# Reordering the first output stage, the first gate products and GpSimd's memsets in a windowed-attention and gated feed-forward kernel

## Chip, core and metric

The kernel runs on one core of a Trainium2 chip. Its time is the device time of one execution in microseconds (us); lower is better. TensorE (PE) does matrix products, VectorE (DVE) and ScalarE (ACT) work on their results in PSUM, GpSimd (POOL) casts, copies and clears in SBUF and issues some loads, SyncE (SP) issues the other loads, the stores and the transposing transfers.

## What is computed

```
scores = q k^T / 8                       # 8 batches x 8 heads, 576 tokens, head size 64
heads 0-3: keep 0 <= i-j < 32
heads 4-7: keep 0 <= i-j < 128 and (i-j) % 4 == 0
x = softmax(scores) v                    # to 4608 tokens x 512
out = (gelu(x w_gate) * (x w_val)) w_out # 512 -> 1536 -> 512
```

Inputs and output are float32; the products run on float16.

## The kernel before

**Units.** Two heads of one batch are one attention unit; unit n belongs to batch n // 4, and units of a batch are plain (heads 0-3) or dilated (heads 4-7). Unit n's steps have letters: S scores (TensorE), P exponential (ScalarE), M mask multiply (VectorE), D denominators and N numerators (TensorE), A or T and B the reciprocal of the denominators (A: two ScalarE passes, `lg` and `rb`; T, B: VectorE), X the multiply that writes x transposed into `xT[pair(n)]` (VectorE, L627). Unit 7 is the last unit of batch 1 and writes `xT[3]`.

**Chunks.** The feed-forward part goes over nine chunks of 512 tokens. A chunk has a gate stage and an output stage. The gate stage has 12 column blocks of 128; each takes four products of 128x512 for the gate and four for the value (`ffn1_part`, L636, one for each `xT`), then `g` (ScalarE, GELU, L801) and `u` (VectorE, L806). Blocks use two pairs of PSUM banks in turn, 0, 1 and 2, 3. The output stage has four blocks of 128 tokens with 12 products each (`ffn2`, L643) and a store (`e`: ScalarE copies, SyncE sends). The 12 products of a block use `wo` in three pieces, four products each.

**Order.** The order on all engines is written out by hand. `gates[c]` and `outs[c]` are strings of words: a number issues so many feed-forward products, and a word such as `S6@2+S7@6` issues steps of units with the PSUM place that they use (for D and N, 0 is banks 4 and 5, 1 is banks 6 and 7 in chunk 0's output stage). Attention of the next batch is thus laid between the output stage's products. `firsts[c]` gives the order of the first 16 gate-stage products, each as block, gate (0) or value (1), and which `xT`. `out_list` gives the order of output products and `out_banks` their banks.

**Loads.** `load_w` and `load_wo` issue the weights from GpSimd's queue. `load_first` (word F) loads q and k of a batch to `stage` from SyncE's queue and casts them on GpSimd (L221 plain heads, L233 dilated heads); `load_rest` (word H) transposes them by transfer (L273), loads v, copies k into block form on GpSimd (L289, L281, L327) and casts v (L262). [...] In chunk 0's output stage the word `V1` calls `second_v`: clear two tiles of batch 2, set `ones_two`, cast batch 1's v, and clear v tiles of batches 2 and 3 (`zero`, L206). A gate on the v loads of batch 1 lets them start once the second piece of `wo` has landed.

Of the kernel before, what the change touches and what calls it, by code (L numbers as in the profile page):

```python
# [21 lines left out]
def kernel(  # L22
# [22 lines left out]
    NNB = DFF // P  # L45
# [102 lines left out]
    def load_w(*parts):  # L148

        for i in parts:  # L150
            for t, w in ((wg_t, moe_w_gate), (wv_t, moe_w_val)):
                src = w[:, WC[i][0] : WC[i][1]].rearrange("(kc p) n -> p kc n", p=P)
                nc.gpsimd.dma_start(out=t[i], in_=src)  # L153

    def load_wo(i):
        return nc.gpsimd.dma_start(  # L156
            out=wo_t[i], in_=moe_w_out[i * CH : (i + 1) * CH, :].rearrange("(fc p) m -> p fc m", p=P)
        )
# [9 lines left out]
    def sixes(src, b):  # L168

        return src[b, 0:HK, :, :].rearrange("h (p r) d -> p h (r d)", r=6)  # L170

    def load_eights(b, pairs=((0, HK),)):
        for h0, h1 in pairs:
            for t, src in zip(eight(b), (q, k)):
                rows_ = src[b, HK + h0 : HK + h1, :, :].rearrange("h (p r) d -> p h (r d)", r=8)
                nc.gpsimd.dma_start(out=t[:, h0:h1].rearrange("p h r d -> p h (r d)"), in_=rows_)  # L176

    def blocks(t, plain):

        return t[:, (1 - plain) * 2 * NB2 * P : (2 - plain) * 2 * NB2 * P].rearrange("p (e c) -> p e c", c=P)  # L180

    def views(b):

        raw = qraw[b % 2]
        kt = raw[:, 1280 + 8 * NCL :]
        return (
            raw[:, 0:1280].rearrange("p (g c) -> p g c", g=2),
            raw[:, 1280 : 1280 + 8 * NCL].rearrange("p (g r i) -> p g r i", g=2, r=4),
            blocks(kt, 1),
            blocks(kt, 0),  # L190
            blocks(vraw[b % 3], 1),
            blocks(vraw[b % 3], 0),
        )
# [5 lines left out]
    def zero(t, eng=nc.gpsimd, gs=(0, 1), swap=1):  # L199

        for x in range(2):
            g = gs[0]
            part = t[64 * x : 64 * x + 64].bitcast(F32)
            first = 32 - 32 * (x ^ (g * swap))
            step = NB2 * 64 + swap * (32 if x else -32) * (1 - 2 * g)
            eng.memset(at2(part[:, NB2 * g], first, [[step, len(gs)], [64, NB2], [1, 32]]), 0.0)  # L206

    def st_of(i):
        return stage[:, 1280 * i : 1280 * i + 1280]
# [46 lines left out]
    def cast_v(dst, i, gs=(0, 1), swap=1):  # L256

        st = st_of(i)[:, 0:1152].rearrange("p (e d) -> p e d", d=D)
        for g in gs:
            for x in range(2):  # L260
                at = slice(NB2 * g, NB2 * g + NB2)
                nc.gpsimd.tensor_copy(dst[half_of(x), at, half_of(x, g * swap)], st[half_of(x), at])  # L262

    def half_of(x, swap=0):
        y = x ^ (1 if swap else 0)
        return slice(64 * y, 64 * y + 64)

    def odd(n):

        return n % 2 if n >= NHP else 0  # L270
# [370 lines left out]
    def ffn2(c, tb, bank, fcs):  # L641
        for fc in fcs:
            nc.tensor.matmul(  # L643
                ps[:, bank, :],
                u_all[:, fc, tb * P : (tb + 1) * P],
                wo_t[fc // 4][:, fc % 4, :],
                start=(fc == 0),
                stop=(fc == NNB - 1),
            )
# [75 lines left out]
    def second():  # L725

        load_w(4)
        for t in views(1)[2:]:
            zero(t)
        for t, src in ((0, q), (1, k)):  # L730
            nc.gpsimd.dma_start(out=six[:, t].rearrange("p h r d -> p h (r d)"), in_=sixes(src, 1))  # L731
        load_w(5)
        load_eights(1)
        wo1 = [load_wo(i) for i in range(3)][1]
        two_masks()
        tiles["two", 1] = views(1)
        gate["dma"] = wo1
        load_v(1, 1, True)
        load_v(1, 2, False)

    def second_v():
        for t in views(2)[2:4]:
            zero(t)
        nc.gpsimd.memset(ones_two, 0.0)
        for x in range(2):
            nc.gpsimd.memset(ones_two[half_of(x), half_of(x, 1)], 1.0)
        cast_v(views(1)[4], 1)
        cast_v(views(1)[5], 2)
        for t in views(2)[4:] + views(3)[5:]:
            zero(t)  # L750
        zero(views(3)[4], gs=(1,))

    def gate_banks(c, nb):

        if c == 0 and nb < 2:
            return ((4, 5), (6, 7))[nb]
        low = ((0, 1), (2, 3))
        return low[(nb + c) % 2]
# [14 lines left out]
    def out_list(c, banks):  # L773
        order = [(tb, fc) for tb in range(4) for fc in range(NNB)]
        if c == 0:
            order[: 2 * NNB] = [(tb, 4 * i + fc) for i in range(3) for tb in range(2) for fc in range(4)]
        return [lambda tb=tb, fc=fc: ffn2(c, tb, banks[tb], fcs=(fc,)) for tb, fc in order]

    def out_banks(c):
        return gate_banks(c, 2) * 2 if c < 7 else (4, 5, 6, 7)  # L780

    def run_program(c, words, mms, banks):

        units = {"S": two_s, "M": two_m, "D": two_den, "N": two_num, "T": two_t, "B": two_b, "X": two_x, "A": two_a, "P": two_p_of, "t": turn_first, "c": cast_six, "W": idle, "b": bias_first}
        joint = {"S": two_s_mms, "D": two_den_mms, "N": two_num_mms}
        for word in words.split():
            kind, args = word[0], [] if "+" in word else [int(x) for x in word[1:].split("@") if x]
            if "+" in word:
                lists = []
                for part in word.split("+"):  # L790
                    n, at = (int(x) for x in part[1:].split("@"))
                    lists.append((joint[part[0]](n, at), odd(n)))
                emit_tiles(*lists)
            elif kind.isdigit():
                for _ in range(int(word)):
                    mms.pop(0)()
            elif kind in units:
                units[kind](*args)
            elif kind == "g":
                g = ffn.tile([P, CH], F16, tag="g")  # L800
                nc.scalar.activation(g, ps[:, gate_banks(c, args[0])[0], :], AF.Gelu)  # L801
                tiles["g", args[0]] = g
            elif kind == "u":
                nb = args[0]
                val = ps[:, gate_banks(c, nb)[1], :]
                nc.vector.scalar_tensor_tensor(u_all[:, nb, :], tiles.pop(("g", nb)), USCALE, val, ALU.mult, ALU.mult)  # L806
            elif kind in "ew":
                at = args[1] if len(args) > 1 else c
                store(at, args[0], out_banks(at)[args[0]], "act" if kind == "e" else "dve")
            elif kind == "L":  # L810
                mms.clear()
                last_block(c, 3, banks[3])
            elif kind == "V":
                second_v() if args else second()
            elif kind == "F":
                load_first(args[0])
            elif kind == "H":
                load_rest(args[0])
            elif kind == "R":
                load_rest(3)  # L820
                load_first(4)
                load_rest(4)
            elif kind == "E":
                nc.scalar.preload_act_table_set("natural_log_exp_and_others")
            else:
                nc.scalar.preload_act_table_set("gelu_and_others")
        assert not mms
# [7 lines left out]
        ),  # L835
        1: (
            "5 N7@0 e3@0 F3 1 X7 1 G 7 g0 2 g1 1 u0 2 u1 2 g2 4 u2 4 g3 4 u3 4 g4 4 u4 4 g5 4 u5 4 g6 4 u6 4 g7 4 "
            "u7 4 g8 4 u8 4 g9 4 u9 4 g10 4 u10 4 g11 3"
        ),
        2: (  # L840
            "5 N11@1 e3@1 R 1 X11 G 7 g0 3 g1 u0 3 u1 2 g2 4 u2 4 g3 4 u3 4 g4 4 u4 4 g5 4 u5 4 g6 4 u6 4 g7 4 u7 "
# [23 lines left out]
    }  # L865
    outs = {
        0: (
            "V1 F2 S4@4+S5@6 1 E P4 10 P5 1 M4 S6@2+S7@6 M5 1 P6 3 D4@0 P7 M6 3 T4 2 e0@0 3 M7 1 e1@0 H2 2 B4 8 "
            "N4@1+D5@0 1 A5 X4 5 N5@0+D6@1 e2@0 1 A6 X5 5 N6@1+D7@0 1 A7 X6"
        ),  # L870
        1: (
            "1 u11 5 S8@0+S9@6 1 E P8 10 P9 M8 1 S10@0+S11@4 e0@1 M9 1 P10 4 P11 D8@1 M10 2 A8 1 M11 3 N8@0+D9@1 "
# [22 lines left out]
        ),  # L895
    }
    firsts = {
# [48 lines left out]
```

## Time and profile before

| | |
|---|---|
| median of 4 runs | 332.54 us (331.93 to 333.34) |
| profiled execution | 332.75 us, span 331.1 us |
| TensorE busy | 323.9 us of the span (98%) |
| VectorE, ScalarE, GpSimd busy | 150.9, 163.3, 149.5 us |
| 128x512 product, booked | 379 to 380 ns, 1284 of them |
| chunk 0: first gate product; first output product | 17.66 us; 42.73 us |
| chunk 1: first gate product; first output product | 56.63 us; 77.91 us |

Times in the profile are from the span's start. A row names the start, the busy time, the engine, the line, the operation with its operands and how many were merged; in brackets stands the idle time of the engine before it and what ended that idle time. The ends of matrix products are modelled. For transfers, SPq rows show the issue; the landing is reported apart, counted from the start of the issue.

### The profile page before, as it was taken

How to read it: one execution, taken by the hardware profiler on the slowest of the kernel's cores; microseconds unless marked ns; L12 is line 12 of the kernel's file. 1: busy time of each engine (PE TensorE's matmuls, PEld its weight loads, DVE VectorE, ACT ScalarE, POOL GpSimd, SP SyncE). 2: the span in 40 equal slices, each digit the busy share in tenths (PEclk: the TensorE clock that was granted, in tenths of full speed). 3: DMA queues.
4: the chain of work that ended last, by engine and by line, in shares of the span. 5: the costliest groups of instructions: out<-in, count | busy, mean ns of one | idle time of the engine just before them, and what ended most of it. 6: DMA issues, size and time to landing. Idle time of an engine off the chain costs nothing.

```text
span 331.1 us, 7540 instructions
## 1 busy us (share of the span) xinstructions
PE 323.9 (98%) x3040; PEld 158.4 (48%) x3040; DVE 150.9 (46%) x226; ACT 163.3 (49%) x246; POOL 149.5 (45%) x246
## 2 busy tenths in 40 slices
PE   7899999999999999999999999999999999999996
PEld 5654545444544454445544454444444444444443
DVE  6763654444443344344434459437743533303320
ACT  2663566535763577347733793356334543213322
POOL 8799877748445755736835941466000000000000
DMA  8999996797798999979789636965000110020002
GB/s 186 188 191 179 203 169 156 190 208 194 187 271 194 178 214 187 248 185 213 198 213 250 154 114 153 239 152 160 34 0 4 65 63 0 0 97 32 0 32 97
DMA packets 109027, 47.98 MB, mean 145 GB/s; under 512 B 83648, under 2 KB 104512, under 8 KB 108992
## 3 DMA queue, kind: packets, MB, share of 16 engines
q1 hardware_dynamic: 97216, 40.06, 51.4%
q0 software_dynamic: 11216, 6.79, 14.4%
q10 hardware_dynamic: 560, 0.66, 0.7%
q8 instruction: 24, 0.39, 0.5%
q14 instruction: 11, 0.09, 0.1%
HBM read 37.75 MB, written 9.44 MB: 143 GB/s over the span
## 4 chain that ended last, share of the span: by engine, by line
PE 85%; POOL 7%; DMA 7%; issue 0%; DVE 0%; POOLq 0%
PE ps L636 50%; PE ps L643 27%; PE ps L457 5%; DMA wo<-in_moe_w_out_dram 5%; DMA xT<-in_k_dram 2%; POOL wv L153 1%; PE ps L446 1%; POOL xT L176 1%; POOL wg L153 1%; POOL v L262 1%; PE ps L667 1%; POOL v L206 1%; POOL q L206 1%; POOL wo L156 0%; POOL s L731 0%
## 5 line engine op out<-in xcount | busy, mean ns | idle before, releaser
L806 DVE SCALAR_TENSOR_TENSOR u_all<-g,ps 128x512 f16<-128x512 f16 x108 | 73.6, 685 | 99.9 <-PE ps L636 92.9
L801 ACT ACTIVATE g<-ps 128x512 f16<-128x512 f32 x108 | 64.0, 598 | 109.2 <-PE ps L636 109.2
L636 PE MATMUL ps<-xT,wg 128*128 128x512 f16 x432 | 114.8, 379 | 0.2 <-DVE xT L627 0.2
L636 PE MATMUL ps<-xT,wv 128*128 128x512 f16 x432 | 113.3, 379 | 0.0
L643 PE MATMUL ps<-wo,u_all 128*128 128x512 f16 x420 | 98.8, 380 | 0.5 <-DMA wo<-in_moe_w_out_dram 0.5
L636 PEld LDWEIGHTS <-wv 128*128 128x128 f16 x432 | 42.1, 98 | 49.7
L636 PEld LDWEIGHTS <-wg 128*128 128x128 f16 x432 | 42.1, 98 | 49.7 <-issue 0.8
L643 PEld LDWEIGHTS <-u_all 128*128 128x128 f16 x420 | 38.3, 98 | 42.8 <-issue 0.8
L262 POOL CAST v<-stage 64x576 f16<-64x576 f32 x60 | 41.9, 698 | 8.5 <-DMA stage<-in_v_dram 5.6
L627 DVE TENSOR_TENSOR xT<-ps,rb 128x576 f16<-128x576 f32 x32 | 29.8, 940 | 23.3 <-PE ps L457 15.4
L221 POOL CAST s<-stage 128x640 f16<-128x640 f32 x24 | 16.9, 731 | 36.7 <-DMA stage<-in_q_dram 25.4
L508 ACT ACTIVATE P<-ps 128x832 f16<-128x832 f32 (+1 forms) x32 | 25.4, 836 | 15.1 <-PE ps L457 12.3
L654 ACT ACTIVATE osb<-ps 128x512 f32<-128x512 f32 x34 | 20.2, 595 | 20.4 <-PE ps L643 20.1
L289 POOL COPY q<-dense 64x1152 f16<-64x1152 f16 (+1 forms) x28 | 20.3, 726 | 15.3 <-DMA dense<-s 14.9
L281 POOL COPY q<-dense 64x512 f16<-64x512 f16 x28 | 17.1, 636 | 5.3 <-DMA dense<-s 3.7
L606 ACT ACTIVATE lg<-ps 128x576 f32<-128x576 f32 x23 | 15.0, 653 | 9.0 <-PE ps L457 8.6
L233 POOL CAST s<-stage 128x512 f16<-128x512 f32 x24 | 14.5, 631 | 9.7 <-DMA stage<-in_q_dram 6.1
L608 ACT ACTIVATE rb<-lg 128x576 f32<-128x576 f32 x23 | 15.8, 686 | 0.7
L513 DVE TENSOR_TENSOR P<-P,two_d 128x768 f16<-128x768 f16 x14 | 9.5, 682 | 13.8 <-ACT P L508 13.1
L513 DVE TENSOR_TENSOR P<-P,two_p 128x832 f16<-128x832 f16 x14 | 10.5, 760 | 11.2 <-ACT P L508 11.1
L457 PEld LDWEIGHTS <-v 64*64 64x64 f16 x460 | 9.2, 107 | 8.3 <-issue 7.0
L457 PE MATMUL ps<-P,v 64*64 64x96 f16 (+5 forms) x460 | 11.2, 199 | 0.0
(81 smaller groups left out, 181.4 us busy)
## 6 DMA issues: line engine op xcount, KB each, us to landing
out_dram<-osb SPq DMA_DIRECT2D x35, 256.0 KB, 2.8
stage<-in_v_dram SPq DMA_DIRECT2D x32, 144.0 KB, 3.6
stage<-in_v_dram SPq DMA_DIRECT2D x28, 128.0 KB, 3.1
stage<-in_q_dram SPq DMA_DIRECT2D x24, 128.0 KB, 3.9
stage<-in_k_dram SPq DMA_DIRECT2D x24, 128.0 KB, 2.9
stage<-in_q_dram SPq DMA_DIRECT2D x6, 512.0 KB, 4.5
stage<-in_k_dram SPq DMA_DIRECT2D x6, 512.0 KB, 5.3
wg<-in_moe_w_gate_dram POOLq DMA_DIRECT2D x6, 256.0 KB, 6.6
```

Source lines behind the costliest of these rows:

```text
L262: nc.gpsimd.tensor_copy(dst[half_of(x), at, half_of(x, g * swap)], st[half_of(x), at])
L281: eng.tensor_copy(dst[half, :, :, half_of(x, g)], src[half])
L289: nc.gpsimd.tensor_copy(out_, src[half].rearrange("p g (j c) -> p g j c", c=64))
L457: nc.tensor.matmul(o[cols], lhs[rows, cols], rhs[rows], start=st, stop=end, skip_group_check=True)
L508: nc.scalar.activation(pt[:, 0 : src.shape[1]], src, AF.Exp, bias=0.0, scale=scale)
L513: nc.vector.tensor_tensor(pt, pt, mask, ALU.mult)
L627: nc.vector.tensor_tensor(dst, num, rb, ALU.mult)
L636: nc.tensor.matmul(ps[:, bank, :], w[:, kc, ns], xT[kc][:, tok], start=first, stop=end)
L643: nc.tensor.matmul(ps[:, bank, :], u_all[:, fc, tb * P : (tb + 1) * P], wo_t[fc // 4][:, fc % 4, :], start=(fc == 0), stop=(fc == NNB - 1),)
L654: nc.scalar.activation(osb, ps[:, bank, :], AF.Copy, bias=0.0, scale=1.0 / USCALE)
L801: nc.scalar.activation(g, ps[:, gate_banks(c, args[0])[0], :], AF.Gelu)
L806: nc.vector.scalar_tensor_tensor(u_all[:, nb, :], tiles.pop(("g", nb)), USCALE, val, ALU.mult, ALU.mult)
```

## The change

It has five parts. In the gate stage of chunk 0, the value products of blocks 0 and 1 that need `xT[0]` and `xT[2]` go ahead of the products that need `xT[1]` and `xT[3]`. In the output stage of chunk 0, three token blocks instead of two go through the `wo` pieces together (36 products instead of 24), block 2 accumulates in bank 2 instead of bank 0, S6 is placed in banks 4 and 5 instead of 2 and 3, and the attention words and stores between the products move accordingly. In the gate stage of chunk 1, N7 is issued after 4 products instead of 5, and `xT[3]`'s first product becomes the twelfth instead of the thirteenth. The eight v memsets at the end of `second_v` become `blank_v`, which the new word `V2` calls after batch 2's `load_first` and ahead of its `load_rest`.

```diff
         cast_v(views(1)[4], 1)
         cast_v(views(1)[5], 2)
+
+    def blank_v():
         for t in views(2)[4:] + views(3)[5:]:
             zero(t)
         zero(views(3)[4], gs=(1,))
...
         if c == 0:
-            order[: 2 * NNB] = [(tb, 4 * i + fc) for i in range(3) for tb in range(2) for fc in range(4)]
+            order[: 3 * NNB] = [(tb, 4 * i + fc) for i in range(3) for tb in range(3) for fc in range(4)]
...
     def out_banks(c):
+        if c == 0:
+            return (0, 1, 2, 1)
         return gate_banks(c, 2) * 2 if c < 7 else (4, 5, 6, 7)
...
             elif kind == "V":
-                second_v() if args else second()
+                (second, second_v, blank_v)[args[0] if args else 0]()
...
     gates 1:
-            "5 N7@0 e3@0 F3 1 X7 1 G 7 g0 2 g1 1 u0 2 u1 2 g2 4 ...
+            "4 N7@0 1 e3@0 F3 1 X7 1 G 6 g0 3 g1 1 u0 2 u1 2 g2 4 ...
...
     outs 0:
-            "V1 F2 S4@4+S5@6 1 E P4 10 P5 1 M4 S6@2+S7@6 M5 1 P6 3 D4@0 P7 M6 3 T4 2 e0@0 3 M7 1 e1@0 H2 2 B4 8 "
-            "N4@1+D5@0 1 A5 X4 5 N5@0+D6@1 e2@0 1 A6 X5 5 N6@1+D7@0 1 A7 X6"
+            "V1 F2 S4@4+S5@6 1 E P4 10 P5 1 M4 S6@4+S7@6 M5 1 P6 5 D4@0 P7 M6 2 T4 5 M7 2 B4 1 e0@0 4 e1@0 V2 H2 "
+            "3 N4@1+D5@0 1 A5 X4 5 N5@0+D6@1 e2@0 1 A6 X5 5 N6@1+D7@0 1 A7 X6"
...
     firsts = {
-        0: "000 100 002 102 001 101 010 110 012 112 011 111 003 103 013 113",
-        1: "000 001 010 011 100 002 012 101 102 110 111 112 003 013 103 113",
+        0: "000 100 002 102 010 110 012 112 001 101 011 111 003 103 013 113",
+        1: "000 001 010 011 100 002 012 101 102 110 111 003 112 013 103 113",
```

More of the change, by code (lines that the diff above doesn't have):

```diff
@@ L836 @@
         1: (
-            "5 N7@0 e3@0 F3 1 X7 1 G 7 g0 2 g1 1 u0 2 u1 2 g2 4 u2 4 g3 4 u3 4 g4 4 u4 4 g5 4 u5 4 g6 4 u6 4 g7 4 "
-            "u7 4 g8 4 u8 4 g9 4 u9 4 g10 4 u10 4 g11 3"
+            "4 N7@0 1 e3@0 F3 1 X7 1 G 6 g0 3 g1 1 u0 2 u1 2 g2 4 u2 4 g3 4 u3 4 g4 4 u4 4 g5 4 u5 4 g6 4 u6 4 g7 "
+            "4 u7 4 g8 4 u8 4 g9 4 u9 4 g10 4 u10 4 g11 3"
         ),
```

## The prediction

> **What bounds the kernel now.** I read the page's totals first, then the waits of TensorE, then TensorE's own timeline around the three places that the diff touches, then the timelines of GpSimd and of SyncE's DMA queue from 50 to 80 us. The totals say that TensorE is the bound, and the granted clock is 1.00 in every stretch that I asked for:
>
> ```profile
> PE 323.9 (98%) x3040; PEld 158.4 (48%) x3040; DVE 150.9 (46%) x226; ACT 163.3 (49%) x246; POOL 149.5 (45%) x246
> ```
>
> So only a hole in TensorE's stream can be won, and a new hole costs in full. Between 15 and 80 us its waits are (us in total, times, longest):
>
> ```profile
> PE ps L643 <- DMA wo<-in_moe_w_out_dram: 0.5, 2, 0.2
> PE ps L446 <- ACT lg L606: 0.3, 1, 0.3
> PE ps L636 <- DVE xT L627: 0.2, 1, 0.2
> ```
>
> The timeline of TensorE shows these holes, and a fourth, before 60.65, that the list lacks; the ACT row beside it is its cause (start us, busy us, engine, line, operation, count, idle before):
>
> ```profile
> 18.81 0.81 PE L636 MATMUL ps<-xT,wg 128*128 128x512 f16 x3
> 19.77 0.59 PE L636 MATMUL ps<-xT,wg 128*128 128x512 f16 x2 [0.15 <-DVE xT L627]
> ...
> 42.73 1.90 PE L643 MATMUL ps<-wo,u_all 128*128 128x512 f16 x8
> 44.86 1.02 PE L643 MATMUL ps<-wo,u_all 128*128 128x512 f16 x4 [0.23 <-DMA wo<-in_moe_w_out_dram]
> 45.81 0.54 PE L457 MATMUL ps<-q 64*64 64x96 f16 x36
> 46.28 1.04 PE L643 MATMUL ps<-wo,u_all 128*128 128x512 f16 x4
> 47.16 0.52 PE L446 MATMUL ps<-P,two_ones 128*128 128x384 f16 x5
> 47.92 4.26 PE L643 MATMUL ps<-wo,u_all 128*128 128x512 f16 x19 [0.24 <-DMA wo<-in_moe_w_out_dram]
> ...
> 60.00 1.09 ACT L801 ACTIVATE g<-ps 128x512 f16<-128x512 f32 x2 [0.20 <-PE ps L636]
> ...
> 60.23 0.38 PE L636 MATMUL ps<-xT,wv 128*128 128x512 f16 x1
> 60.65 1.02 PE L636 MATMUL ps<-xT,wg 128*128 128x512 f16 x4
> ```
>
> **How large the holes are: a row against a rule.** The idle column gives 0.15 + 0.23 + 0.24 us, with some 0.04 before 60.65 that the chain shows as "issue": 0.66 us, 0.2% of the span. But one such product is booked at 379 ns, while 80 of them in the same gate stage start from 60.65 to 77.91: 0.2158 us each. The Trainium skill, "Perfetto Trace Analysis", section "Tensor Engine Instruction (MATMUL, LD_WEIGHTS)", says that a matmul's end in the profile is estimated from its size and not observed, so a difference of an end and a start is not the lost time. I count from start to start. Three products from 18.81 would let the next start at 19.46; it starts at 19.77: 0.31. Eight from 42.73 end at 44.46; next 44.86: 0.40. D4 with its change-over takes 0.37 (D8, a stage later: products due at 84.04 and 84.41), so after four products from 46.28 the next is due at 47.51; it starts at 47.92: 0.40. After 60.23 the next is due at 60.45; 60.65: 0.20. Sum 1.31 us. By the booked idle the change could win 0.66, by the starts 1.31; I take the starts.
>
> **The change, part by part.** No matmul, cast, memset or transfer is added or removed; all is order, but for two bank numbers and where eight memsets stand.
>
> Gate stage 0: four value and gate products of units 0 and 2 now stand before the first one of unit 1. Unit 1's X multiply starts at 18.96 and lasts 0.76, to 19.72. The product that waited for it is due at 19.46 + 4 x 0.2158 = 20.32: the 0.31 is gone. Unit 3's X ends at 20.74; its first product comes at 21.19. The values now start at 19.46 and need wv's first piece: issued 12.24, landed after 6.6, 18.84. Cover 0.6. Everything PE-paced after it is 0.31 earlier; the later weight pieces land earlier still, the nearest being k's eights (issued 30.11, 8.8 to landing: 38.9, needed from about 39.6).
>
> Output stage 0: before, 8 products use wo's first piece, then 8 and 8; now 12, 12, 12. The pieces are issued at 30.84, 31.62, 32.34 and land after 11.5, 13.2, 15.5: 42.3, 44.8, 47.9, and nothing in the change moves them. The first product is due at 42.42: on the edge, a wait of 0 to 0.1; I take 0. Twelve end at 45.01; S6 and S7 take 0.56 with their change-over (45.72 to 46.28 before). The second piece is needed at 45.5 (landed 44.8), six products go to 46.87, D4 to 47.24, six more to 48.5, and there the third piece is needed (47.9). Both 0.40 holes go. The first product of gate stage 1 moves from 56.63 to 56.63 - 0.31 - 0.80 = 55.52.
>
> New waits in this stretch. S6 moves from bank 2 to bank 4, so it waits for P4, and D4, which stands in bank 4 too, for P6; behind D4 in TensorE's queue stand 30 products. P4 and P5 end at 44.7 (45.0 less 0.31), S6 comes at 45.0, and S7 waited for P5 already. P6 began 0.66 after S6 in before and lasts 0.76: free 1.42 after S6; D4 comes 0.56 + 6 x 0.2158 = 1.85 after: cover 0.4. Block 2 in bank 2 meets only its own store, done before gate stage 1 wants the bank; block 3 in bank 1 starts 4 products and N4 after block 1's last product, 1.4 us, against a store of about 0.25 + 0.6. The thinnest cover is v: GpSimd's casts at 53.34 hang on SyncE's loads, which hang on wo's second piece and so do not move. The second of them ends at 54.72, and N6, before at 55.93, is now due at 54.82. The v casts of N4, N5 and N7 leave 0.8, 0.7 and 0.2. DVE hands X1 to TensorE in 0.05 (19.72 to 19.77), so the value is 0, the bounds 0 and 0.3.
>
> Gate stage 1: N7 and so X7 come one product earlier, product (0, gate, 3) is twelfth instead of thirteenth, and g0 is free to start 0.22 earlier against its stage. That product started at 59.59 and g0 at 60.00; now 58.27 and 58.68. The table load ended 0.21 before g0 in before, 58.67 now, so it just stops short of being the wait. g0 at 58.69 frees bank 2 at 59.34 (0.65 later, as before); the product that needs it is due at 59.34. The 0.20 is gone: 60.65 becomes 59.34. X7 ends 1.74 after N7's start, at 58.12, before 58.27.
>
> GpSimd's eight memsets, 4.36 us, go behind the q and k casts of batch 2. This wins nothing itself: it pays for what is late next. S8 needs the last copy of batch 2:
>
> ```profile
> 56.23 4.36 POOL L206 MEMSET v<- 64x576 f32 x8
> 60.65 2.81 POOL L221 CAST s<-stage 128x640 f16<-128x640 f32 x4
> ...
> 67.83 1.17 POOL L233 CAST s<-stage 128x512 f16<-128x512 f32 x2 [2.18 <-DMA stage<-in_k_dram]
> 71.64 2.34 POOL L289 COPY q<-dense 64x1152 f16<-64x1152 f16 x2 [2.63 <-DMA dense<-s]
> 75.73 1.16 POOL L281 COPY q<-dense 64x512 f16<-64x512 f16 x2 [1.75 <-DMA dense<-s]
> ...
> 78.64 0.29 POOL L327 COPY q<-q 128x128 f16<-128x128 f16 x1
> ...
> 60.25 0.55 SPq L228 DMA_DIRECT2D stage<-in_q_dram  x1
> 62.05 0.37 SPq L228 DMA_DIRECT2D stage<-in_k_dram  x1
> ```
>
> The copy ends at 78.93 and S8 starts at 79.30: cover 0.37. TensorE 1.31 earlier would find S8 0.9 short. Now walk the new order. q's plain pieces landed by 54.98 + 3.6 = 58.6, so their casts run 58.65 to 60.05. SyncE is ready for k's dilated load at 60.80; in before it stood there until the cast freed the stage at 62.03. It goes 1.2 us earlier, and in SyncE's queue the two stores and four transposes behind it go 1.2 earlier. Where q and k are issued 0.7 apart (89.9, 117.9, 145.2) they land 1.4 to 1.6 apart, here, 1.8 apart, 3.4. So k lands at 64.35 + 1.5 = 65.9, or, at its old 5.7, at 66.55. Casts to 67.1 (67.8); memsets, now in the idle time ahead of the copies, to 71.5 (72.2); plain copies to 73.9 (74.6); the last transpose, landed 75.7 before, 74.5 now; 3.2 more: last copy at 77.7 (77.8). S8 is due at 77.98. Wait 0, with bounds 0 and 1.1 (k landing at its old 67.75 puts the last copy at 79.0).
>
> Downstream nothing is near: batch 3's copies end at 108.4 for 114.1, and TensorE has no wait left after 60.65. VectorE and ScalarE are 46% and 49% busy. Sum: -0.31 - 0.40 - 0.40 - 0.20 = -1.31. The profiled execution took 332.75 (331.1 span and 1.65 around it), so 331.44; it stands 0.2 above the median of 332.54, so 331.2 against the median.
>
> **The rivals.** (a) Covers half fail: N6 waits for v, wo's first piece is late, the table load takes over as g0's wait, or S8 waits for its copy by up to 1.1. Total gain 0.2 to 0.9, 331.6 to 332.3. For it: four covers under 0.3 us in a row. Against: the moved chain is anchored to rows, and two routes to k's landing give the same end.
>
> (b) Slower: the memsets as GpSimd's new bound. They now stand between k's cast and S8's copies, so from k's landing L the last copy is at L + 0.05 + 1.2 + 4.4 + 2.4 + 3.2 = L + 11.25. From L = 66.7 S8 waits; at 68.0 the gain is used up; at 69.0 the kernel is 1.0 slower; at 69.7, 334.2. L = 69.0 is 8.1 us after issue. Against: the eight such loads I looked at landed 4.1 to 5.7 after issue.
>
> (c) The change doesn't do what it says in gate stage 0: another wait, such as the "ACT lg" one at 18.32 that the diff leaves alone, sets the time there, and the 0.31 stays. Then the gain is 1.0, 331.5. Against: X1 ends at 19.72 and the waiting product starts at 19.77, so the hole is X1's.
>
> **Numbers.** 1.31 whole or nearly: 0.66. Rival (a): 0.20. Rival (b): 0.10, nearly all of it past the point where it costs 1.0. Rival (c): 0.04, half to each side of the bound. A measurement of this kernel can tell about 0.3%, 1.0 us, from no change, so faster means below 331.54: 0.66 + 0.02 = 0.68; slower 0.09; same the rest, 0.23. The range: 330.7 (the sum and half a microsecond of the runs' own spread) to 332.4 (the upper end of (a)).
>
> **What would show it.** TensorE waits for wo and for xT gone; gate stage 1's first product at 55.5, the first product of gate block 2 at 59.3; the last GpSimd copy at 77.7 and S8 at 78.0; the tail 1.3 earlier. The forecast is wrong if N6 or S8 shows a GpSimd wait, or D4 an ACT one.

## The result and the profile after

The changed kernel takes 331.47 us (median of 42 runs, 330.88 to 333.05) against 332.62 us (64 runs). The ratio of the runs is 0.9974, with a 95% interval of 0.9967 to 0.9981: 0.86 us less, between 0.63 and 1.10. (The medians alone differ by 1.15.) Two more measurements beside the experiments gave 0.9975 both. The profiled execution took 331.48 us with a span of 329.8, which is 1.27 below the profiled execution of before (1.3 by the spans).

The page of the changed kernel, totals, and TensorE's waits between 15 and 80 us (us in total, times, longest). The L446 wait is in the prologue, at 15.6:

```profile
PE 322.9 (98%) x3040; PEld 158.1 (48%) x3040; DVE 152.0 (46%) x226; ACT 163.4 (50%) x246; POOL 150.2 (46%) x246
...
PE ps L643 <- DMA wo<-in_moe_w_out_dram: 0.3, 1, 0.3
PE ps L446 <- POOL v L262: 0.2, 1, 0.2
```

The timelines of TensorE and ScalarE at the same places as before; the PEld row is the weight load ahead of the product at 19.02:

```profile
18.29 0.81 PE L636 MATMUL ps<-xT,wg 128*128 128x512 f16 x3
19.02 1.04 PE L636 MATMUL ps<-xT,wv 128*128 128x512 f16 x4
19.01 0.55 PEld L636 LDWEIGHTS <-wv 128*128 128x128 f16 x4 [0.41 <-DMA wv<-in_moe_w_val_dram]
19.89 0.59 PE L636 MATMUL ps<-xT,wg 128*128 128x512 f16 x2
...
41.51 0.56 PE L457 MATMUL ps<-q 64*64 64x96 f16 x36
42.36 2.75 PE L643 MATMUL ps<-wo,u_all 128*128 128x512 f16 x12 [0.28 <-DMA wo<-in_moe_w_out_dram]
45.51 1.47 PE L643 MATMUL ps<-wo,u_all 128*128 128x512 f16 x6
46.81 0.52 PE L446 MATMUL ps<-P,two_ones 128*128 128x384 f16 x5
47.19 3.83 PE L643 MATMUL ps<-wo,u_all 128*128 128x512 f16 x17
...
58.70 1.22 ACT L805 ACTIVATE g<-ps 128x512 f16<-128x512 f32 x2
...
59.13 0.38 PE L636 MATMUL ps<-xT,wv 128*128 128x512 f16 x1
59.35 1.02 PE L636 MATMUL ps<-xT,wg 128*128 128x512 f16 x4
```

The four holes are gone: no product of the first gate stage waits for unit 1's X, the waits for the second and the third piece of `wo` do not occur, and gate block 2 starts at 59.35 with g0 at 58.70. Two waits are new. A small one: the first value product is due at 18.94 and starts at 19.02, because `wv`'s first piece, issued at 11.3, lands 7.7 later, at 19.0. A larger one: the first output product. S4 and S5 let the next product start at 42.00 (0.49 after their start, as in profiles without a wait), and `wo`'s first piece lands at 42.3 (issued 30.8, 11.5 to landing): 0.36 us of TensorE from start to start. The landings themselves did not move.

GpSimd, SyncE's queue and TensorE around S8:

```profile
58.91 1.38 POOL L221 CAST s<-stage 128x640 f16<-128x640 f32 x2 [2.69 <-DMA stage<-in_q_dram]
64.81 2.47 POOL L233 CAST s<-stage 128x512 f16<-128x512 f32 x4 [2.02 <-PE ps L636]
67.22 4.36 POOL L206 MEMSET v<- 64x576 f32 x8
71.62 2.32 POOL L289 COPY q<-dense 64x1152 f16<-64x1152 f16 x2
74.00 1.16 POOL L281 COPY q<-dense 64x512 f16<-64x512 f16 x2
76.92 0.29 POOL L327 COPY q<-q 128x128 f16<-128x128 f16 x1
...
60.31 0.37 SPq L228 DMA_DIRECT2D stage<-in_k_dram  x1
...
78.00 0.54 PE L457 MATMUL ps<-q 64*64 64x96 f16 x36
```

The memsets now fill the time in which GpSimd waited for the transposes. k's dilated load goes at 60.31 instead of 62.05, the last copy for S8 ends at 77.21 instead of 78.93, and S8 starts at 78.00 instead of 79.30.

### The profile page after: what moved, and what is told of

Read it like the earlier page. It is cut to its first block, busy times and chain, and to the rows that moved or that the text cites. A ratio compares the mean times of both kernels' runs of the same rounds, so it can differ in the third digit from the quotient of the medians.

```text
span 329.8 us, 7539 instructions
## 1 busy us (share of the span) xinstructions
PE 322.9 (98%) x3040; PEld 158.1 (48%) x3040; DVE 152.0 (46%) x226; ACT 163.4 (50%) x246; POOL 150.2 (46%) x246
## 4 chain that ended last, share of the span: by engine, by line
PE 86%; DMA 7%; POOL 4%; SPq 1%; issue 0%; DVE 0%; POOLq 0%
PE ps L636 50%; PE ps L643 29%; PE ps L457 5%; DMA wo<-in_moe_w_out_dram 3%; DMA stage<-in_v_dram 2%; DMA u_all<-in_q_dram 2%; PE ps L446 1%; POOL wv L153 1%; POOL wg L153 1%; PE ps L667 1%; POOL q L206 1%; POOL v L206 1%; SPq L245 1%; POOL xT L176 0%; POOL s L731 0%; POOL v L262 0%
## 5 line engine op out<-in xcount | busy, mean ns | idle before, releaser
L643 PEld LDWEIGHTS <-u_all 128*128 128x128 f16 x420 | 38.3, 98 | 42.3 <-issue 0.3
L262 POOL CAST v<-stage 64x576 f16<-64x576 f32 x60 | 41.7, 695 | 10.9 <-DMA stage<-in_v_dram 8.0
L221 POOL CAST s<-stage 128x640 f16<-128x640 f32 x24 | 17.7, 764 | 40.3 <-DMA stage<-in_q_dram 27.9
L513 DVE TENSOR_TENSOR P<-P,two_d 128x768 f16<-128x768 f16 x14 | 11.2, 815 | 13.6 <-ACT P L508 13.2
L457 PE MATMUL ps<-P,v 64*64 64x96 f16 (+5 forms) x460 | 11.3, 199 | 0.0
```

The costliest lines, as they stand in the source:

```text
L221: nc.gpsimd.tensor_copy(s16[:, 1280 * t + 640 * g : 1280 * t + 640 * g + 640].rearrange("p (k c) -> p k c", k=5), st_of(i).rearrange("p (k ...
L457: nc.tensor.matmul(o[cols], lhs[rows, cols], rhs[rows], start=st, stop=end, skip_group_check=True)
L513: nc.vector.tensor_tensor(pt, pt, mask, ALU.mult)
L643: nc.tensor.matmul(ps[:, bank, :], u_all[:, fc, tb * P : (tb + 1) * P], wo_t[fc // 4][:, fc % 4, :], start=(fc == 0), stop=(fc == NNB - 1),)
```

## The experiments

Times are given as the ratio to the kernel before with its 95% interval; 0.001 is 0.33 us. The changed kernel stands at 0.9974 or 0.9975. All experiments are edits of it except where another base is named. A distance from the changed kernel is the difference of the two ratios, since each kernel ran beside the kernel before; the medians alone, taken on different chips, can give a few tenths of a microsecond more or less. One profile is one execution; where its time is far from the median, it is given.

### Each part undone

**Two blocks per piece.**

```diff
-order[: 3 * NNB] = [... for i in range(3) for tb in range(3) for fc in range(4)]
+order[: 2 * NNB] = [... for i in range(3) for tb in range(2) for fc in range(4)]
```

> The changed kernel with only two token blocks sharing each wo piece again (8, 8, 8 products), attention words and banks as changed. Theory A (the landings of wo's pieces at 42.3, 44.8 and 47.85 bind): first product at 42.36, the ninth waits from 44.1 to 44.85, the seventeenth from 47.15 to 47.9, and D4 no longer lies in that hole; the first product of gate stage 1 at 57.0 instead of 55.5, time 1.5 more than the changed kernel: 332.9, a little above before. Rival B (the order of the output products is worth little, the gain came from the other parts): under 0.5 more, 331.9 at most.

Measured 332.66 us, 1.0013 (1.0002 to 1.0024): 1.3 us above the changed kernel (0.9 to 1.2 by the medians). Theory A holds by the time: without this one line the other parts bring nothing. The line is needed, but 1.3 is not its worth by itself: the attention words stay where they suit three blocks, and on the kernel before the whole output stage's part brings 0.3, not clear of nothing (below). Theory A's reason for a time even above before, that D4 no longer lies inside the wait, is argued and not shown: the profiled execution (333.00 us) has no such waits, since in it TensorE came to the output stage only at 43.9 (see the last section), and the pieces, landed at 42.1, 44.8 and 47.6, were each there before their first product.

```profile
43.93 2.76 PE L643 MATMUL ps<-wo,u_all 128*128 128x512 f16 x12
```

**Gate stage 0 back.**

```diff
-0: "000 100 002 102 010 110 012 112 001 101 011 111 003 103 013 113",
+0: "000 100 002 102 001 101 010 110 012 112 011 111 003 103 013 113",
```

> The changed kernel with the old order of the first 16 products of chunk 0's gate stage. Theory A (X1's hole of 0.31 is part of the gain): a hole of 0.2 to 0.3 between the fourth and fifth product again, and everything behind it as much later: 331.8. Rival B (the landing of the first wo piece at 42.3 is the bound of the output stage now, so what gate stage 0 wins is waited away there): the X1 hole is back, the wait for wo at 42.36 shrinks by as much, the first output product stays at 42.36 to 42.5, time 331.5.

Measured 331.79 us, 0.9989 (0.9980 to 0.9998), 0.5 above the changed kernel by the ratios (0.05 to 0.3 by the medians), with intervals that just overlap. In the profiled execution (331.20 us, the lowest of its 22) the first piece had landed at 41.0 (issued 30.1, 10.9 to landing), so nothing waited there, and X1's hole (18.85 due, 19.17 started: 0.32) counted in full. The timeline of TensorE:

```profile
18.20 0.81 PE L636 MATMUL ps<-xT,wg 128*128 128x512 f16 x3
19.17 0.59 PE L636 MATMUL ps<-xT,wg 128*128 128x512 f16 x2 [0.16 <-DVE xT L627]
...
42.12 2.76 PE L643 MATMUL ps<-wo,u_all 128*128 128x512 f16 x12
```

So rival B, as a rule for all executions, is wrong: whether the hole counts depends on where the first piece lands.

**Gate stage 0 alone,** on the kernel before (the same line, the other way).

> The kernel before with the new order of chunk 0's first 16 gate products alone. Theory A (in the kernel before, the third wo piece's landing sets the time of the output stage, so an earlier arrival is waited away): the X1 hole is gone and the wo waits grow by as much, 1.000 of before. Rival B (the hole counts by itself): 0.31 less, 0.9991.

Measured 332.50 us, 1.0001 (0.9992 to 1.0010): nothing. The timeline of TensorE in the profiled execution (331.41 us, the lowest of its 22) shows where such a gain ends:

```profile
18.05 0.81 PE L636 MATMUL ps<-xT,wg 128*128 128x512 f16 x3
18.70 1.03 PE L636 MATMUL ps<-xT,wv 128*128 128x512 f16 x4
...
41.69 1.89 PE L643 MATMUL ps<-wo,u_all 128*128 128x512 f16 x8
43.78 1.02 PE L643 MATMUL ps<-wo,u_all 128*128 128x512 f16 x4 [0.20 <-DMA wo<-in_moe_w_out_dram]
46.07 0.52 PE L446 MATMUL ps<-P,two_ones 128*128 128x384 f16 x5
46.57 4.26 PE L643 MATMUL ps<-wo,u_all 128*128 128x512 f16 x19
```

X1's hole is gone, and TensorE waits at the ninth product (43.42 due, 43.78) and at the seventeenth (46.44 due, 46.57; the third piece landed at 31.8 + 14.7 = 46.5). The growth of the waits that was expected is not seen: they are 0.36 and 0.13, against 0.40 and 0.40 in the profile of the kernel before, since in this execution the pieces were issued some 0.5 us earlier. But with X1's hole of 0.31 the ninth product would have been due at 43.73, still before 43.78, so nothing behind it would have come later. In the kernel before, a part that only brings TensorE to `wo` earlier is waited away.

**N7 back.**

```diff
-1: "4 N7@0 1 e3@0 F3 1 X7 1 G 6 g0 3 g1 ..."   and 003 as twelfth
+1: "5 N7@0 e3@0 F3 1 X7 1 G 7 g0 2 g1 ..."     and 003 as thirteenth
```

> The changed kernel with N7 after five products of chunk 1's gate stage again and product (0, gate, 3) as the thirteenth. Theory A (g0 comes one product too late for bank 2): a hole of 0.2 before the first product of gate block 2, 59.55 instead of 59.35; time 0.2 more, 331.7. Rival B (g0 is set by the table load, not by the product): no hole, 331.5.

Measured 331.51 us, 0.9974 (0.9959 to 0.9988). The time does not resolve 0.2 us. The timeline does: the product that needs g0's bank is due at 59.21 and starts at 59.41, so the hole is back as theory A says.

```profile
58.99 0.38 PE L636 MATMUL ps<-xT,wv 128*128 128x512 f16 x1
59.41 1.02 PE L636 MATMUL ps<-xT,wg 128*128 128x512 f16 x4
```

**Memsets back.**

```diff
-... 4 e1@0 V2 H2 ...      # blank_v after the casts of q and k
+... 4 e1@0 H2 ...         # its memsets at the end of second_v again
```

> The changed kernel with the eight v memsets back ahead of the q and k casts of batch 2; all else as changed. Theory A (the memsets' place is what lets S8 follow TensorE's earlier arrival): the casts of q start at about 60.6, k's dilated load goes at 62.0 instead of 60.3, the last copy for S8 ends at 78.9 instead of 77.2, S8 starts at 78.9 to 79.0 instead of 78.0 with a GpSimd wait before it; time 0.9 to 1.0 above the changed kernel, about 332.4, 0.9994 of before. Rival B (S8's copies hang on the transposes whatever GpSimd does before, and are in time): S8 at 78.0, 331.5, 0.9967.

Measured 331.73 us, 0.9983 (0.9972 to 0.9994): 0.3 above the changed kernel where 0.9 to 1.0 was expected, and the intervals overlap. GpSimd and TensorE in its profile:

```profile
66.86 1.18 POOL L233 CAST s<-stage 128x512 f16<-128x512 f32 x2 [1.78 <-DMA stage<-in_k_dram]
77.85 0.29 POOL L327 COPY q<-q 128x128 f16<-128x128 f16 x1
...
76.78 1.46 PE L643 MATMUL ps<-wo,u_all 128*128 128x512 f16 x6
78.17 0.54 PE L457 MATMUL ps<-q 64*64 64x96 f16 x36
...
53.33 1.47 PE L643 MATMUL ps<-wo,u_all 128*128 128x512 f16 x6
55.47 0.39 PE L643 MATMUL ps<-wo,u_all 128*128 128x512 f16 x1
```

The last copy ends at 78.14, and S8 starts at 78.17, when its sixth product lets it: no wait, and no cover. Two things let it come out even. k's load, issued at 62.29, landed after about 4.5 us and not after 5.7. And N6 had waited 0.27 for v (from block 3's six products to its last one 2.14, against 1.87 without a wait); without that S8 would have been due at 77.90, 0.24 before its copy. So the memsets' place buys cover, 0.79 us in the changed kernel's profile against 0.03 here; that it also bought time is not shown.

### One part alone, one cost doubled

**The output stage alone,** on the kernel before: the three-block order, its banks and its words, memsets in front.

> The kernel before with the output stage's part alone: three blocks per wo piece, the banks and the words of that stage; memsets ahead of the casts, gate stages 0 and 1 as before. Theory A (the wo holes are won, then mostly given back at S8): the wo waits go but for the first piece's, the hole before gate block 2 stays, S8 waits for its copy until about 78.9 to 79.0 where it could start at 78.2 to 78.5; gain 0.3 to 0.4: 332.2. Rival B (S8's cover does not run out): gain 0.8 to 1.1: 331.6.

Measured 332.25 us, 0.9992 (0.9982 to 1.0003), the number of theory A, but not for its reason. S8 starts at 78.88 as soon as its sixth product allows, with its copy done at 78.50. What TensorE waited for is v: N5 should follow six products from 51.70, which with N5 take 1.91; the next product is at 54.11, so 0.50 is lost to the cast that ends at 53.55. Without that loss S8 would have been due at 78.38, 0.12 before its copy.

```profile
51.70 1.47 PE L643 MATMUL ps<-wo,u_all 128*128 128x512 f16 x6
54.11 1.47 PE L643 MATMUL ps<-wo,u_all 128*128 128x512 f16 x6
...
52.16 1.39 POOL L262 CAST v<-stage 64x576 f16<-64x576 f32 x2 [1.20 <-DMA stage<-in_v_dram]
```

**The memsets twice.**

```diff
         zero(views(3)[4], gs=(1,))
+        for t in views(2)[4:] + views(3)[5:]:
+            zero(t)
+        zero(views(3)[4], gs=(1,))
```

> The changed kernel with the eight memsets done twice in their new place (4.36 us more on GpSimd, results the same). This sizes the rival of the prediction that had the memsets as GpSimd's new bound. Theory A (the last copy hangs on casts, memsets, copies in a row, 0.75 ahead of S8): the last copy ends at 81.6, S8 starts at 81.6 instead of 78.0, time 3.6 more: 335.1, 1.0075. Rival B (the copies hang on the transposes with idle time before them): 2.5 more or less, 334.0 at most.

Measured 336.66 us, 1.0123 (1.0101 to 1.0145): 4.9 us above the changed kernel. The profiled execution is the lowest of its six, 335.23. The chain is that of theory A, since the copies follow the memsets without a gap and end at 80.72, but the time is 1.3 above its 3.6. GpSimd's and TensorE's timelines, and the busy time of TensorE and its granted clock (the column after POOL's) in three stretches:

```profile
66.20 8.89 POOL L206 MEMSET v<- 64x576 f32 x16
75.13 2.32 POOL L289 COPY q<-dense 64x1152 f16<-64x1152 f16 x2
80.43 0.29 POOL L327 COPY q<-q 128x128 f16<-128x128 f16 x1
...
76.16 1.46 PE L643 MATMUL ps<-wo,u_all 128*128 128x512 f16 x6
78.17 0.23 PE L457 MATMUL ps<-q 64*64 64x96 f16 x1 [0.56 <-POOL q L281]
79.62 0.23 PE L457 MATMUL ps<-q 64*64 64x96 f16 x2 [1.22 <-POOL q L281]
80.18 1.12 PE L457 MATMUL ps<-q 64*64 64x96 f16 x33 [0.33 <-POOL q L281]
81.23 3.76 PE L643 MATMUL ps<-wo,u_all 128*128 128x512 f16 x12
84.93 0.56 PE L457 MATMUL ps<-q 64*64 64x96 f16 x36
...
78.00:80.00 2.00, 0.46 (x3) 0.21 (x3) 0.00 (x0) 0.00 (x0) 1.96 (x5) 0.97 1.07 260
80.00:82.00 2.00, 1.76 (x35) 1.01 (x36) 0.00 (x0) 0.67 (x1) 1.88 (x5) 0.50 1.09 271
82.00:84.00 2.00, 2.00 (x8) 0.78 (x7) 1.83 (x2) 1.10 (x3) 1.82 (x4) 0.68 0.70 144
```

S8 is due at 77.55, and but for three short products it waits for its copies until 80.18: 2.6 us. After the wait the clock stands at 0.50 and 0.68. The rest of S8 takes 1.05 us (81.23 less 80.18), where all of S8 takes 0.47 at 1.00, though its last copy, at 80.72, may hold it too. The step of twelve products from 81.23 to 84.93 takes 3.70 us instead of the 2.70 that it takes at 1.00. So in this execution the wait of some 2.6 us costs a further 1.0 to 1.6 us. That it is the wait that brings the clock down fits the other executions: of the six, five have a mean granted clock of 0.990 to 0.995 over the whole kernel, against two of 22 of the changed kernel beside them.

### The next bounds

**The first piece in halves; the order of the v loads; both.** `wo`'s first piece is loaded by two transfers and its twelve products go by halves (e5); the two small rest loads of v go ahead of the second pair of dilated heads (e10); both (e9).

```diff
...
+            order[:12] = [(tb, 2 * j + fc) for j in range(2) for tb in range(3) for fc in range(2)]
...
-        for x in range(2 - 2 * plain):          # rest loads after both pairs
+            for x in range(2 - 2 * g):          # rest loads after the first pair
```

> The changed kernel with wo's first piece loaded as two halves (one transfer more in GpSimd's queue) and the first twelve products ordered by halves. Theory A (the first piece's landing is a bound, but the v loads, which are tied to wo's second piece, are the next one 0.3 behind it): first output product at 42.0 or as early as TensorE arrives, then N6 waits for its v cast that ends at 54.8; gain against the changed kernel 0 to 0.1: 331.4. Rival B (the landing is the only bound): gain 0.3 to 0.4: 331.1. Rival C (the extra transfer delays the later pieces): 0.2 to 0.5 slower than the changed kernel.

> The changed kernel with the order of the v loads alone. Theory A (N6's v cast is a bound in some executions only): the cast ends 1.2 earlier, at about 53.5, N6 starts 0.1 behind its sixth product in any case; time 0.0 to 0.2 below the changed kernel. Rival B: nothing, or the second pair's cast, now last, holds N7: 0.1 above.

> The changed kernel with wo's first piece in two halves, and in the v loads of dilated heads the two small rest loads ahead of the second pair of heads instead of behind it, so that N6's cast needs four loads instead of six. Theory A (the first wo landing and N6's v cast are the next two bounds, 0.0 to 0.4 and 0.0 to 0.3): 0.2 to 0.5 below the changed kernel, 331.1 to 331.3, and no TensorE wait for wo or GpSimd between 41 and 57. Rival B (N5, N7 or the table load take their place at once): the same as the changed kernel, 331.5.

Measured: halves 331.22 us, 0.9972 (0.9958 to 0.9987); v order 331.49, 0.9978 (0.9968 to 0.9987); both 331.22, 0.9966 (0.9953 to 0.9980). In the profile of both, TensorE meets neither wait: the first half has landed by 40.2, S4 to the first product is 41.62 to 42.11, and N4 to N7 follow their products at once. Both together have the lowest ratio, 0.3 us below the changed kernel, and the same median as the halves, but the intervals overlap, so a gain is not shown. Inconclusive.

**The changed kernel again.**

> The changed kernel itself, next to the others of this call on the same chip. Theory A (all of the moved holes are TensorE's): 0.9965, about 1.15 to 1.3 us below before. Rival B (part of the first measurement was chance): within 0.3 of before.

> The changed kernel itself beside these three on the same chip: 0.9975 of before. It serves as their scale; it also shows whether the waits for wo's first piece and for N6's v cast come and go between executions, as theory A has it (wo wait 0 to 0.4, N6 0 to 0.3).

Measured 331.64 us, 0.9975 (0.9965 to 0.9986), and 331.74, 0.9975 (0.9963 to 0.9987): 0.8 us below before, so the gain itself is no chance, but the 1.15 to 1.3 of theory A lies at the far end of both intervals or beyond it. In three profiles of one kernel the wait for the first piece was 0.36, 0.45 and 0.36 us from start to start, and the stretch from block 3's six products to its last one 1.94, 2.00 and 1.87: N6's wait for v was 0.07, 0.13 and 0. Four experiments have the same program up to the first output product: there the wait for the first piece was 0.12 (memsets back), 0.21 (N7 back) and none (memsets twice; v order, where TensorE came late). So these waits do change between executions.

## Why the prediction was right, and where it was not

**Right, by its steps.** The size of a hole read from start to start: the pair of profiled executions differs by 1.27, against 1.31 by the starts and 0.66 by the booked idle time. Inside one profile, where a shift of the prologue drops out, the steps agree as well. From the first output product to the first gate product of chunk 1 it is 13.90 us before and 13.17 after: 0.73 of the predicted 0.80, and N6's wait for v is the missing 0.07. From there to gate block 2 it is 4.02 and 3.82: the 0.20. S6 and D4 on banks 4 and 5 meet no ScalarE wait. k's load goes 1.7 us earlier (predicted 1.2) and lands at 66.0, between the two predictions of 65.9 and 66.55.

**Luck: the absolute times.** 55.52 was predicted for the first gate product of chunk 1 and 55.53 measured; 59.34 and 59.35 for gate block 2; 77.98 and 78.00 for S8. These hang on the first output product, predicted at 42.42 and measured at 42.36. TensorE was ready for it at 42.00, since the prologue of that execution, which the change does not touch, was 0.52 faster (second gate product at 18.29 instead of 18.81), and 0.08 of that went to `wv`'s first piece, for which a cover of 0.6 had been predicted. The wait for `wo`'s first piece took the rest back.

**Mis-sized: the 0.31 of gate stage 0.** The hole itself went, so rival (c) is out: no other wait held its place. But its worth is not 0.31 in every execution. Alone on the kernel before it is nothing (1.0001), as there the second and third landing set the pace. In the changed kernel the first landing can set it: "a wait of 0 to 0.1; I take 0" became 0.36 to 0.45 in three profiles and 0 to 0.21 in four others with the same program up to there. Where the wait is over 0.31, the earlier arrival is waited away whole; where there is none, it counts in full. An estimate from these seven waits, 0.31 less the wait but not below nothing, gives a mean of 0.13; the experiment that takes the part back, 0.05 to 0.5 us, cannot settle it. The error was to read one margin, 42.42 against 42.3, off a single execution: TensorE's second gate product varies from 18.05 to 19.10 among the profiles with an undisturbed clock, the first landing from 41.0 to 42.7 among all that load the piece in one transfer.

**Mis-sized: the 0.80 for `wo`'s two holes.** It is the distance between landings less TensorE's work between them, and that is a matter of the execution: 0.40 and 0.40 in the one that was read, 0.36 and 0.13 in the one of "gate stage 0 alone". That fits a mean gain of 0.86 below 1.31; how the missing 0.45 divides between this, X1 and v was not settled.

**Rival (a), in part.** "1.31 whole or nearly" describes the pair of profiles, but it lies outside the interval of the runs, 0.63 to 1.10. The mean of 0.86 is the upper end of rival (a), 0.2 to 0.9, and two of the failing covers that (a) names did occur: `wo`'s first piece came late, and N6 waited for v. The other two, the table load and S8's copy, held.

**Overrated: S8's shortfall of 0.9.** It rested on one landing of k (5.7 us). With the memsets back the copy was in time, with 0.03 to spare and with the help of a wait elsewhere. Rival (b), which had the memsets as the new bound, was a sound picture: with 4.5 us more of them S8 is late. But its threshold was far, 0.79 us of cover, and its price was too low, as the clock comes on top.

**Right in kind: the thinnest cover is v.** It was put at 0 with bounds 0 and 0.3; N6 lost 0.07 in the changed kernel's profile, 0.13 in its second, 0.27 with the memsets back, and N5 0.50 in the output stage's part alone.

The greatest chance was on a time below 331.54, a gain over 0.3%. The median of 331.47 is just below it; the ratio's 0.26% falls a little short.

## What to carry to other kernels

Measure a hole in TensorE's stream from start to start against the pace of the products around it, and where a transfer's landing sets the time of what waits for it, take an earlier arrival of the engine as worth only what exceeds that wait. When weights land in pieces, share each piece among more output blocks until the work per piece, with what is laid between, covers the distance between landings: here, from the first use of one piece to that of the next, 1.7 and 2.7 us of products and attention before, 3.2 and 3.0 after, against landings 2.5 and 3.1 us apart. A sum of holes taken from one profiled execution is a sum for that execution; where a hole is a race between two streams, its mean over runs can be smaller than one reading of it suggests.

## What was not expected of the hardware

With the memsets twice, a wait of some 2.6 us in the middle of the kernel left TensorE at a granted clock of 0.50 and 0.68 in the two stretches behind it, 80 to 84 us. A wait of 0.4 us did not: the clock of the changed kernel is 1.00 from 19 to 60 us, with the wait at 42.36 in it. A low clock comes in some prologues too, without a cause in the edits: in the profile of "two blocks per piece" three stretches read:

```profile
10.00:12.00 2.00, 1.47 (x37) 1.23 (x33) 1.92 (x4) 1.13 (x2) 1.18 (x2) 1.00 1.40 192
12.00:14.00 2.00, 1.57 (x37) 1.35 (x38) 1.93 (x4) 0.42 (x2) 1.33 (x2) 0.72 1.41 198
14.00:17.00 3.00, 3.00 (x52) 2.35 (x50) 1.04 (x4) 1.40 (x2) 2.88 (x5) 0.62 1.48 190
```

Its first gate product comes at 19.19 instead of 17.6. The v order's profile has the same (0.63 and 0.68, 18.83). Why some prologues fall into it was not tried.
